# A ring of four weight and cache slots as one tile, with merged weight transfers

## The chip, the cores and the metric

The kernel runs on one core of a Trainium2 chip. The metric is the device time of one execution in microseconds; lower is better. TensorE (PE) does the matrix products, VectorE (DVE) the element-wise work, reductions and 32x32 block transposes, ScalarE (ACT) activations and copies, GpSimd (POOL) the memsets at the start, and SyncE (SP) issues almost all transfers. Sixteen DMA engines move the data from HBM to the on-chip memory.

## The reference

One decoding step for two sequences. A normalised input row feeds two branches: a windowed attention over cached keys and values (32 query heads, 8 key/value heads, a window of 4096 positions), and a small gated MLP. Their product is added to the input.

```python
xn = _layernorm(x)                                   # x: (2, 1, 512)
# attention
q = (xn @ wq).reshape(2, 1, 32, 128)                 # wq: (512, 4096)
k = k_cache[:, :, Sk - 4096:, :]                     # (2, 8, 4096, 128), each used by 4 heads
v = v_cache[:, :, Sk - 4096:, :]
p = softmax(einsum(q, k) * 128 ** -0.5)
s = einsum(p, v).reshape(2, 1, 4096) @ wo            # wo: (4096, 512)
# gated MLP
z = gelu(xn @ w_in)                                  # w_in: (512, 1792)
z1, z2 = z[..., :896], _layernorm(z[..., 896:])
g = silu((z1 * (w_sp * z2 + b_sp)) @ w_out)          # w_out: (896, 512)
return x + s * g
```

All data are float32. The keys and values in the window are 67 MB, w_q and w_o 8.4 MB each, w_in 3.7 MB and w_out 1.8 MB; each is read once.

## The kernel before

**Units.** The cache is worked in eight units (`NU`, L69): a unit is one sequence and two key/value heads, and its keys are one tile of 128 partitions by 64 positions by 128 (32 KB a partition, 4 MB), its values another. `load_unit` (L114) issues one transfer for one of them.

**The ring.** All large data go through the pool `ring` (L76), four buffers of 32 KB a partition (`SLOT`, L73). `slot` (L81) takes the next buffer in turn, and the transfer that fills it waits until every reader of the tile that was there has finished. In order of turns: w_in, w_out, the two halves of w_q, then k0, k1, v0, k2, v1, k3, v2 and so on to k7, v6, v7, and three buffers for w_o. All these transfers stand on SP, in this order; the loop at L416 issues those of the cache, the loop at L426 those of w_o.

**w_q.** Two transfers (L101 to L104), each of two of the four rows that a partition holds: 32 KB of every 64 KB. The q matmuls (L274 to L281) run over k = 0..3, eight groups of four for each k pair; those of k = 0, 1 read the first half and those of k = 2, 3 the second.

**w_o.** 32 blocks of 512 columns a partition (64 KB a partition in all). They come in pieces of 8, 8, 8, 4, 2, 1 and 1 blocks (`pieces`, L424), a transfer each; the first two pieces share one buffer, the third has one, the last four share one. After the second piece one small transfer brings `x4` (L434), which is x spread over eight partitions.

**Order of work.** Every engine runs its instructions in the order in which the program writes them (`InOrder`, L27); an instruction that waits holds up all behind it on its engine. SP holds nothing but transfers. The sequence is: layer norm and MLP branch up to `gate` (L145 to L270), the q matmuls, `qT`, `qm`, `rp` and `qbd` (L273 to L296, DVE and PE in turn), and then the loop over units (L438 to L464). In it DVE turns a unit's keys in four chunks (`turn`, tile `kt`), PE multiplies each chunk with q (`shares`, tile `sh`), ACT copies it, PE adds the shares up (`add_shares`, tile `s`); in between, for the unit before, the maximum, the exponentials (`p`), their transposes (`pT`) and the products with the values (`values`, tile `acc`) are done. So a k buffer is free after the fourth transposition of its unit, and a v buffer after the sixteen products of the next unit's turn.

**The end.** After the last unit (L465 to L477) the heads are gathered into `oT`. Then blocks 0 to 27 of w_o are multiplied into `part` (L482 to L485), ACT copies `part`, and blocks 28 to 31 go into `so` directly, with the copy added in before block 30 (L489 to L497). Two DVE operations and one store finish. In the trace an ordinary block is two matmul instructions of `part`, and one of the last four blocks is eight of `so`.

All engine calls go through one helper, so the profile gives them line 37; they are told apart by the tile that they write.

Of the kernel before, what the change touches and what calls it, by code (L numbers as in the profile page):

```python
# [9 lines left out]
F32 = mybir.dt.float32  # L10
# [4 lines left out]
P = 128  # L15
HQ, DH = 32, 128
G = 4
# [4 lines left out]
def ap(t, offset, dims):  # L22

    return bass.AP(tensor=t.tensor, offset=t.offset + offset, ap=[list(t.ap[0])] + [list(d) for d in dims])
# [18 lines left out]
def kernel(  # L43
# [14 lines left out]
    pe, dve, act, sp = (InOrder(tc, e) for e in (nc.tensor, nc.vector, nc.scalar, nc.sync))  # L58
    B, _, D = x.shape
    _, HKV, SK, _ = k_cache.shape  # L60
    W = min(4096, max(256, SK // 4))
    REP = HQ // HKV
    F = w_in.shape[1]
    FH = F // 2
    KT = D // P
    FT = FH // P
    DC = D // G
    SCALE = DH ** -0.5
    NU = B * HKV // 2  # L69
# [3 lines left out]
    SLOT = J * DH  # L73
    BANKS = {"s": 2, "sh": 2, "acc": 2, "mo": 1, "col": 1}

    ring = ctx.enter_context(tc.tile_pool(name="ring", bufs=4))  # L76
    cst = ctx.enter_context(tc.tile_pool(name="cst", bufs=1))
    sb = ctx.enter_context(tc.tile_pool(name="sb", bufs=2))
    ps = ctx.enter_context(tc.tile_pool(name="ps", bufs=1, space=bass.MemoryType.PSUM))

    def slot(name):  # L81
        return ring.tile([P, SLOT], F32, tag="slot", name=name)

    def const(name, *shape):
        return cst.tile([P, *shape], F32, tag=name, name=name)

    def bank(name, tag):
        return ps.tile([P, 512], F32, tag=tag, name=name, bufs=BANKS[tag])


    xs = cst.tile([B, D], F32, tag="xs", name="xs")
    act.dma_start(xs, x[:, 0, :])
    win = slot("win")[:, : KT * F]
    sp.dma_start(win, w_in.rearrange("(p k) f -> p (k f)", p=P))
    win = win.rearrange("p (k f) -> p k f", k=KT)
    wout = slot("wout")[:, : FT * D]
    sp.dma_start(wout, w_out.rearrange("(p j) d -> p (j d)", p=P))
    wout = wout.rearrange("p (j d) -> p j d", j=FT)
    wq_v = wq.rearrange("(p k) f -> p k f", p=P)
    wqt = []  # L100
    for a in range(2):  # L101
        t = slot(f"wq{a}")
        sp.dma_start(t, wq_v[:, 2 * a : 2 * a + 2, :].rearrange("p k f -> p (k f)"))
        wqt.append(t.rearrange("p (k f) -> p k f", k=2))  # L104

    wb1 = cst.tile([1, 2], F32, tag="wb1", name="wb1")
    act.dma_start(wb1[:, 0:1], bass.AP(tensor=w_sp.tensor, offset=w_sp.offset, ap=[[1, 1], [1, 1]]))
# [2 lines left out]
    def by_group(t):  # L110

        return bass.AP(tensor=t.tensor, offset=t.offset, ap=[[DC, G], [D, B], [1, DC]])

    def load_unit(cache, u, name):  # L114

        b, w = divmod(u, NU // B)
        t = slot(f"{name}{u}")
        first = cache[b, 2 * w, SK - W :, :]
        src = bass.AP(tensor=first.tensor, offset=first.offset, ap=[[SLOT, P // 2], [SK * DH, 2], [1, SLOT]])
        sp.dma_start(t, src)  # L120
        return t.rearrange("p (j d) -> p j d", d=DH)


    ident = const("ident", P)
# [1 line left out]
    xnT = const("xnT", KT, 32)  # L126
# [5 lines left out]
    x4 = const("x4", DC)  # L132
# [70 lines left out]
    for k in range(KT):  # L203
        for g in range(G):
            pe.matmul(
                pz[32 * g : 32 * g + 32, :], xnT[:, k, :], ap(win[:, k, :], g * FQ, [[FH, 2], [1, FQ]]),
                start=(k == 0), stop=(k == KT - 1),
            )
    wb_ps = bank("wb_ps", "mo")[:, :2]
    pe.matmul(wb_ps, ones[0:1, :], wb1, start=True, stop=True)  # L210
    wb = const("wb", 2)
# [46 lines left out]
    for j in range(FT):  # L258
        g = j % G
        pe.matmul(yp[32 * g : 32 * g + 32, :], hT[:, j, :], wout[:, j, :], start=(j < G), stop=(j >= FT - G))  # L260
    ys = sb.tile([P, D], F32, tag="shs", name="ys")
    act.activation(ys, yp, AF.Copy)
    y = bank("yq", "mo")[:, :DC]
# [9 lines left out]
    pq = [bank(f"q_ps{r}", "s") for r in range(2)]  # L273
    for k in range(KT):  # L274
        for r in range(2):
            for g in range(G):
                c = (r * G + g) * 512
                pe.matmul(
                    pq[r][32 * g : 32 * g + 32, :], xnT[:, k, :], wqt[k // 2][:, k % 2, c : c + 512],
                    start=(k == 0), stop=(k == KT - 1),  # L280
                )  # L281
    qT = sb.tile([P, 1024], F32, tag="qT", name="qT", bufs=1)
    for r in range(2):
        dve.transpose(qT[:, 512 * r : 512 * r + 512], pq[r])
# [13 lines left out]
    def q_of(u, dq):  # L298
        return ap(qbd, (u.n * 4 + dq) * 32, [[1, 32]])


    class Unit:
        pass

    def turn(u, m):

        u.kt[m] = sb.tile([P, JC, DH], F32, tag="kt", name=f"kt{u.n}_{m}", bufs=3)
        dve.transpose(
            u.kt[m].rearrange("p j d -> p (j d)"), u.k[:, JC * m : JC * m + JC, :].rearrange("p j d -> p (j d)")
        )  # L310

    def shares(u, m):

        u.sh = bank(f"sh{u.n}_{m}", "sh")
        for dq in range(4):
            pe.matmul(
                u.sh[32 * dq : 32 * dq + 32, :], q_of(u, dq), u.kt[m][:, :, 32 * dq : 32 * dq + 32],
                start=True, stop=True,
            )
        u.shs[m] = sb.tile([P, 512], F32, tag="shs", name=f"shs{u.n}_{m}")  # L320
        act.activation(u.shs[m], u.sh, AF.Copy)

    def add_shares(u, m):

        if m == 0:
            u.s = bank(f"s{u.n}", "s")
        pe.matmul(u.s, add_dq[:, NCH - 1 - m : NCH - 1 - m + P], u.shs[m], start=(m == 0), stop=(m == NCH - 1))
# [24 lines left out]
    def probs_t(u):  # L352
        u.pT = sb.tile([P, JC, 32], F32, tag="pT", name=f"pT{u.n}")
        dve.transpose(u.pT.rearrange("p j r -> p (j r)"), u.p)

    def weights(u):
        pe.matmul(u.mo[:, 32:34], same_r, u.l, start=True, stop=True)
# [8 lines left out]
    def values(u, part=0, parts=1):  # L366
        if part == 0:
            u.acc = bank(f"acc{u.n}", "acc")
        n = JC // parts
        for j in range(n * part, n * part + n):  # L370
            c = j % G
            pe.matmul(
                u.acc[32 * c : 32 * c + 32, :], u.pT[:, j, :], u.v[:, j : J : JC, :],
                start=(j < G), stop=(j >= JC - G),
            )

    def scale_out(u):
        u.o = sb.tile([P, 4, DH], F32, tag="o", name=f"o{u.n}")
        for jj in range(4):
            act.activation(  # L380
                u.o[:, jj, :], u.acc[:, jj * DH : (jj + 1) * DH], AF.Copy, scale=u.wd[:, jj : jj + 1]
            )
# [3 lines left out]
    def collect(u):  # L386

        if u.n == 0:
            col[0] = bank("col", "col")
        r = slice(32 * u.b, 32 * u.b + 32)  # L390
        pe.matmul(
            col[0][r, :], sel[:, 24 - 8 * u.w : 56 - 8 * u.w], u.o.rearrange("p j d -> p (j d)"),
            start=(u.w == 0), stop=(u.w == NU // B - 1),
        )
# [11 lines left out]
            )  # L406
        dve.tensor_copy(oT[:, :, 16 * u.b], t)

    units = []
    for n in range(NU):  # L410
        u = Unit()
        u.n, u.kt, u.shs = n, {}, {}
        u.b, u.w = divmod(n, NU // B)
        units.append(u)

    for n in range(NU + 1):  # L416
        if n < NU:
            units[n].k = load_unit(k_cache, n, "k")
        if n > 0:
            units[n - 1].v = load_unit(v_cache, n - 1, "v")  # L420

    wo_v = wo.rearrange("(p j) d -> p j d", j=32)
    blocks = []
    pieces = ((8, 8), (8,), (4, 2, 1, 1))  # L424
    j = 0
    for i, piece in enumerate(pieces):  # L426
        t = slot(f"wo{i}").rearrange("p (j d) -> p j d", d=D)
        at = 0
        for n in piece:
            sp.dma_start(t[:, at : at + n, :], wo_v[:, j : j + n, :])  # L430
            blocks += [(t, at + a) for a in range(n)]
            at, j = at + n, j + n
            if j == 16:
                sp.dma_start(x4[0:P:16, :], by_group(x))  # L434

    prev = old = None
    last = units[-1]
    for u in units:  # L438
        turn(u, 0)
        shares(u, 0)  # L440
        if old is not None:
            gather(old)
        if prev is not None:
            share_max(prev)
            probs(prev)
            weights(prev)
        turn(u, 1)
        shares(u, 1)
        add_shares(u, 0)
        if prev is not None:  # L450
            probs_t(prev)
            weigh(prev)
            if u is not last:
                values(prev)
        for m in range(2, NCH):
            turn(u, m)
            shares(u, m)
            add_shares(u, m - 1)
        if u is not last and prev is not None:
            scale_out(prev)  # L460
        add_shares(u, NCH - 1)
        if u is not last and prev is not None:
            collect(prev)
        old, prev = prev, u  # L464
    values(old, 0, 2)  # L465
    share_max(last)
    probs(last)
    values(old, 1, 2)
    weights(last)
    probs_t(last)  # L470
    weigh(last)
# [10 lines left out]
    for n in range(EARLY):  # L482
        t, a = blocks[n]
        g = n % G
# [4 lines left out]
    for n in range(EARLY, 32):  # L489
        if n == LATE:  # L490
            spread_quarters(so, parts, start=False, stop=False)
        t, a = blocks[n]
# [37 lines left out]
```

## Time and profile before

| | |
|---|---|
| time of three runs | 217.88, 218.21, 218.34 us (median 218.21) |
| the profiled execution | 217.89 us, of which the span of the trace is 216.1 us |
| mean granted clock of TensorE | 0.854 |
| read from HBM | 89.40 MB, 414 GB/s over the span |
| busy: PE, DVE, ACT | 153.6, 108.6, 44.0 us |
| SP's transfers | 3912 packets |

In the rows of the profile times are in microseconds from the start of the span, unless marked ns. `k<-in_A_k_cache_dram` is what is written and what it is read from; `x32` is a number of instructions; `128x512 f32` is partitions by elements. In the time line and the groups the brackets or the last column tell how long the engine was idle just before, and what ended that. The chain of waits is followed back from the last instruction of the span, at each step to what released it. In the page's slices a digit is the busy share in tenths, 9 for 90% or more.

### The profile page before, as it was taken

The numbers are of one execution on the slowest core, as the hardware profiler recorded it, in microseconds if no ns is written. First come the engines' busy times: TensorE is split into PE (matmuls) and PEld (weight loads), VectorE is DVE, ScalarE is ACT, GpSimd is POOL, SyncE is SP. The second block draws the span as 40 slices with busy tenths as digits, with TensorE's granted clock in tenths as the row PEclk, the third lists the DMA queues.
The fourth block names the chain that finished last, engine by engine and source line by source line (L and its number), as shares of the span: only waits on it lengthen the run. The fifth ranks groups of instructions, "written<-read, shape, count | busy, mean of one in ns | idle before, by whom it ended". The sixth has DMA issues, their size and how long they took to land.

```text
span 216.1 us, 2228 instructions
## 1 busy us (share of the span) xinstructions
PE 153.6 (71%) x866; PEld 43.1 (20%) x866; DVE 108.6 (50%) x176; ACT 44.0 (20%) x109; POOL 2.6 (1%) x14
## 2 busy tenths in 40 slices
PE   0173185518959957994995699459959967997963
PEld 0121121101212212221221222222222212231311
DVE  2505402569788079338806941685479089331001
ACT  5003310002231331043131304120331241242001
POOL 4000000000000000000000000000000000000000
PEclk9998579955997995899799589856996996999698
DMA  6999999999999999999999999999999999999990
GB/s 256 425 437 467 406 438 422 431 443 419 455 400 473 397 455 412 431 437 419 450 403 461 412 461 403 443 419 425 449 412 452 412 455 412 443 397 425 424 368 26
DMA packets 3929, 89.54 MB, mean 414 GB/s; under 512 B 446, under 2 KB 462, under 8 KB 848
## 3 DMA queue, kind: packets, MB, share of 16 engines
q1 hardware_dynamic: 3912, 89.40, 96.7%
q8 instruction: 7, 0.11, 0.2%
q10 hardware_dynamic: 8, 0.00, 0.0%
q14 instruction: 2, 0.02, 0.0%
HBM read 89.40 MB, written 0.00 MB: 414 GB/s over the span
## 4 chain that ended last, share of the span: by engine, by line
DMA 52%; PE 28%; DVE 18%; issue 1%; DVEq 0%; SPq 0%
DMA k<-in_A_k_cache_dram 38%; DVE kt L37 15%; PE sh L37 9%; PE s L37 8%; DMA wo<-in_A_wo_dram 8%; PE acc L37 6%; DMA win<-in_B_w_in_dram 5%; PE z L37 2%; PE mo L37 1%; PE so L37 1%; DVE m L37 1%; DVE pT L37 1%; PE oT L37 0%; DVE mx L37 0%; PE col L37 0%
## 5 line engine op out<-in xcount | busy, mean ns | idle before, releaser
L37 DVE STREAM_TRANSPOSE kt<-k 128x2048 f32<-128x2048 f32 x32 | 72.7, 2295 | 41.7 <-DMA k<-in_A_k_cache_dram 35.7
L37 PE MATMUL sh<-kt,qbd 128*32 128x512 f32 x256 | 41.4, 710 | 18.4 <-DVE kt L37 18.4
L37 ACT ACTIVATE shs<-sh 128x512 f32<-128x512 f32 x32 | 19.1, 597 | 119.3 <-PE sh L37 119.3
L37 PE MATMUL s<-shs,add_dq 128*128 128x512 f32 x64 | 40.0, 732 | 0.0
L37 PE MATMUL acc<-v,pT 128*32 128x512 f32 x256 | 31.9, 640 | 0.2 <-DVE pT L37 0.2
L37 PEld LDWEIGHTS s<-shs,add_dq 128*128 128x128 f32 x64 | 11.0, 215 | 30.1 <-issue 25.7
L37 PEld LDWEIGHTS sh<-kt,qbd 128*32 128x32 f32 x256 | 6.5, 115 | 38.8 <-issue 24.5
L37 PEld LDWEIGHTS acc<-v,pT 128*32 128x32 f32 x256 | 7.7, 119 | 25.5 <-issue 18.3
L37 PE MATMUL mo<-l,same_r 128*128 128x2 f32 x16 | 3.7, 299 | 10.6 <-ACT p L37 10.6
L37 ACT ACTIVATE o<-acc,wd 128x128 f32<-128x128 f32 x32 | 9.1, 372 | 3.4 <-PE acc L37 3.4
L37 PE MATMUL part<-wo,oT 128*32 128x512 f32 x56 | 8.0, 708 | 2.0 <-DMA wo<-in_A_wo_dram 1.7
L37 ACT ACTIVATE p<-s,nb 128x256 f32<-128x256 f32 x16 | 7.6, 490 | 7.2 <-DVE nb L37 6.9
L37 PE MATMUL q_ps<-wq,xnT 128*32 128x512 f32 x64 | 7.3, 594 | 2.3 <-DMA wq<-in_A_wq_dram 2.3
L37 PE MATMUL col<-o,sel 128*32 128x512 f32 x16 | 8.3, 601 | 0.4 <-ACT o L37 0.4
L37 PE MATMUL z<-win,xnT 128*32 128x448 f32 x32 | 5.3, 836 | 4.5 <-DMA win<-in_B_w_in_dram 4.5
L37 DVE TENSOR_REDUCE m<-s 128x2 f32<-128x512 f32 x8 | 5.4, 670 | 4.9 <-PE s L37 4.9
L37 DVE TENSOR_TENSOR res<-so,gate 128x128 f32<-128x128 f32 x1 | 0.3, 291 | 11.7 <-PE so L37 11.7
L37 PE MATMUL y<-wout,hT 128*32 128x512 f32 x14 | 3.3, 993 | 3.8 <-issue 3.8
L37 DVE STREAM_TRANSPOSE pT<-p 128x512 f32<-128x512 f32 x8 | 5.4, 674 | 1.2 <-ACT p L37 1.2
L37 ACT ACT_TABLE_LOAD x4 | 5.1, 1283 | 1.9 <-issue 1.9
L37 PE MATMUL xnT_ps<-ident,xn 2*128 2x2 f32 x4 | 0.6, 252 | 6.9 <-DVE xn L37 6.9
L37 PEld LDWEIGHTS mo<-l,same_r 128*128 128x128 f32 x16 | 3.0, 233 | 12.2 <-ACT p L37 12.2
(106 smaller groups left out, 63.2 us busy)
## 6 DMA issues: line engine op xcount, KB each, us to landing
k<-in_A_k_cache_dram SPq DMA_DIRECT2D x8, 4096.0 KB, 26.0
v<-in_A_v_cache_dram SPq DMA_DIRECT2D x8, 4096.0 KB, 30.6
wq<-in_A_wq_dram SPq DMA_DIRECT2D x2, 4096.0 KB, 29.7
wo<-in_A_wo_dram SPq DMA_DIRECT2D x3, 2048.0 KB
win<-in_B_w_in_dram SPq DMA_DIRECT2D x1, 3584.0 KB
wout<-in_B_w_out_dram SPq DMA_DIRECT2D x1, 1792.0 KB, 15.0
wo<-in_A_wo_dram SPq DMA_DIRECT2D x1, 1024.0 KB
wo<-in_A_wo_dram SPq DMA_DIRECT2D x1, 512.0 KB, 18.0
```

The lines of the kernel that those rows point to most:

```text
L37: return self.tc.keep_in_program_order(call(*args, **kwargs))
```

## The change

The pool `ring` is gone. One tile of 4 x 32 KB a partition, also named `ring`, takes its place, and its four parts are handed out by the program: `enqueue` appends a load with the number of parts that it needs, `advance` marks parts as free and issues loads from the head of the queue as long as their parts are free. `advance` is called behind the last reader of each part. The waits of a transfer come from the parts of the tile that earlier instructions read or wrote.

```diff
-    ring = ctx.enter_context(tc.tile_pool(name="ring", bufs=4))
...
-    def slot(name):
-        return ring.tile([P, SLOT], F32, tag="slot", name=name)
+    ring = cst.tile([P, 4 * SLOT], F32, tag="ring", name="ring")
+    free = [True] * 4
+    queue = []
+    turns = [0]
+
+    def enqueue(load, count=1):
+        at = turns[0] % 4
+        turns[0] += count
+        queue.append((load, range(at, at + count)))
+        advance()
+
+    def advance(*slots):
+        for n in slots:
+            free[n] = True
+        while queue and all(free[n] for n in queue[0][1]):
+            load, at = queue.pop(0)
+            for n in at:
+                free[n] = False
+            load(ring[:, at[0] * SLOT : (at[-1] + 1) * SLOT], at[0])
```

w_q takes two parts at once and comes in one transfer, 64 KB a partition:

```diff
-    wq_v = wq.rearrange("(p k) f -> p k f", p=P)
-    wqt = []
-    for a in range(2):
-        t = slot(f"wq{a}")
-        sp.dma_start(t, wq_v[:, 2 * a : 2 * a + 2, :].rearrange("p k f -> p (k f)"))
-        wqt.append(t.rearrange("p (k f) -> p k f", k=2))
...
+            sp.dma_start(t[:, :n], w.rearrange("(p k) f -> p (k f)", p=P))
+            weight[name] = t[:, :n].rearrange("p (k f) -> p k f", k=k)
...
+    enqueue(load_rows("in", w_in, KT))
+    enqueue(load_rows("out", w_out, FT))
+    enqueue(load_rows("q", wq, KT), 2)
```

w_o comes in pieces of 16, 8, 4, 1, 1, 1 and 1 blocks, the first of them 32 KB a partition, and `x4` in two transfers of four partitions each in place of one of eight:

```diff
-    pieces = ((8, 8), (8,), (4, 2, 1, 1))
...
-                sp.dma_start(x4[0:P:16, :], by_group(x))
...
+            if len(blocks) == 16:
+                for b in range(B):
+                    sp.dma_start(x4[16 * b : P : 32, :], x[b].rearrange("o (g c) -> (o g) c", g=G))
...
+    for piece in ((16,), (8,), (4, 1, 1, 1, 1)):
+        enqueue(load_blocks(piece))
```

The calls that hand parts back: `advance(0)` behind the matmuls of w_in, `advance(1)` behind those of w_out, `advance(2, 3)` behind the q matmuls, `advance(u.slot["k"])` ahead of a unit's last `add_shares`, `advance(prev.slot["v"])` behind it, and `advance(old.slot["v"])` at the end. The order in which loads take the parts is that of the turns before.

More of the change, by code (lines that the diff above doesn't have):

```diff
@@ L92, with load_rows, load @@
     act.dma_start(xs, x[:, 0, :])
[L93 to L98, printed above, removed]
-    wq_v = wq.rearrange("(p k) f -> p k f", p=P)
-    wqt = []
-    for a in range(2):
-        t = slot(f"wq{a}")
-        sp.dma_start(t, wq_v[:, 2 * a : 2 * a + 2, :].rearrange("p k f -> p (k f)"))
-        wqt.append(t.rearrange("p (k f) -> p k f", k=2))
+    weight = {}
+    def load_rows(name, w, k):
+        def load(t, at):
+            n = k * w.shape[1]
+            sp.dma_start(t[:, :n], w.rearrange("(p k) f -> p (k f)", p=P))
+            weight[name] = t[:, :n].rearrange("p (k f) -> p k f", k=k)
+        return load
+    enqueue(load_rows("in", w_in, KT))
+    enqueue(load_rows("out", w_out, FT))
+    enqueue(load_rows("q", wq, KT), 2)
+    win, wout, wqt = (weight[n] for n in ("in", "out", "q"))
     wb1 = cst.tile([1, 2], F32, tag="wb1", name="wb1")
@@ L114, in load_unit, with load, load_blocks @@
     def load_unit(cache, u, name):
-        b, w = divmod(u, NU // B)
-        t = slot(f"{name}{u}")
-        first = cache[b, 2 * w, SK - W :, :]
+        first = cache[u.b, 2 * u.w, SK - W :, :]
         src = bass.AP(tensor=first.tensor, offset=first.offset, ap=[[SLOT, P // 2], [SK * DH, 2], [1, SLOT]])
-        sp.dma_start(t, src)
-        return t.rearrange("p (j d) -> p j d", d=DH)
+        def load(t, at):
+            sp.dma_start(t, src)
+            setattr(u, name, t.rearrange("p (j d) -> p j d", d=DH))
+            u.slot[name] = at
+        return load
+    class Unit:
+        pass
+    units = []
+    for n in range(NU):
+        u = Unit()
+        u.n, u.kt, u.shs, u.slot = n, {}, {}, {}
+        u.b, u.w = divmod(n, NU // B)
+        units.append(u)
+    for n in range(NU + 1):
+        if n < NU:
+            enqueue(load_unit(k_cache, units[n], "k"))
+        if n > 0:
+            enqueue(load_unit(v_cache, units[n - 1], "v"))
+    wo_v = wo.rearrange("(p j) d -> p j d", j=32)
+    blocks = []
+    def load_blocks(piece):
+        def load(t, at):
+            t = t.rearrange("p (j d) -> p j d", d=D)
+            a = 0
+            for n in piece:
+                j = len(blocks)
+                sp.dma_start(t[:, a : a + n, :], wo_v[:, j : j + n, :])
+                blocks.extend((t, a + i) for i in range(n))
+                a += n
+            if len(blocks) == 16:
+                for b in range(B):
+                    sp.dma_start(x4[16 * b : P : 32, :], x[b].rearrange("o (g c) -> (o g) c", g=G))
+        return load
+    for piece in ((16,), (8,), (4, 1, 1, 1, 1)):
+        enqueue(load_blocks(piece))
     ident = const("ident", P)
@@ L208 @@
             )
+    advance(0)
     wb_ps = bank("wb_ps", "mo")[:, :2]
@@ L260 @@
         pe.matmul(yp[32 * g : 32 * g + 32, :], hT[:, j, :], wout[:, j, :], start=(j < G), stop=(j >= FT - G))
+    advance(1)
     ys = sb.tile([P, D], F32, tag="shs", name="ys")
@@ L278 @@
                 pe.matmul(
-                    pq[r][32 * g : 32 * g + 32, :], xnT[:, k, :], wqt[k // 2][:, k % 2, c : c + 512],
+                    pq[r][32 * g : 32 * g + 32, :], xnT[:, k, :], wqt[:, k, c : c + 512],
                     start=(k == 0), stop=(k == KT - 1),
                 )
+    advance(2, 3)
     qT = sb.tile([P, 1024], F32, tag="qT", name="qT", bufs=1)
@@ L299, in q_of @@
         return ap(qbd, (u.n * 4 + dq) * 32, [[1, 32]])
-    class Unit:
-        pass
     def turn(u, m):
@@ L407, in gather @@
         dve.tensor_copy(oT[:, :, 16 * u.b], t)
[L409 to L423, printed above, removed]
-    pieces = ((8, 8), (8,), (4, 2, 1, 1))
[L425 to L433, printed above, removed]
-                sp.dma_start(x4[0:P:16, :], by_group(x))
     prev = old = None
@@ L460 @@
             scale_out(prev)
+        advance(u.slot["k"])
         add_shares(u, NCH - 1)
         if u is not last and prev is not None:
+            advance(prev.slot["v"])
             collect(prev)
@@ L468 @@
     values(old, 1, 2)
+    advance(old.slot["v"])
     weights(last)
```

## The prediction

> **What bounds the kernel now.** I read the page first (busy shares, slices, queues, chain), then the transfers by stage, then the chain in order of time and the time line around the edited places.
>
> ```profile
> span 216.1 us, 2228 instructions
> PE 153.6 (71%) x866; PEld 43.1 (20%) x866; DVE 108.6 (50%) x176; ACT 44.0 (20%) x109; POOL 2.6 (1%) x14
> DMA  6999999999999999999999999999999999999990
> q1 hardware_dynamic: 3912, 89.40, 96.7%
> q8 instruction: 7, 0.11, 0.2%
> DMA 52%; PE 28%; DVE 18%; issue 1%; DVEq 0%; SPq 0%
> ```
>
> No compute engine is above 71%; the 16 DMA engines are in the top tenth in every slice but the first and the last, and SP's queue (q1) alone fills 96.7% of them. The next rows are stretches of the span; the last column is GB/s, the one before it the DMA share.
>
> ```profile
> 1.80:37.40 35.60, 14.66 (x100) 5.22 (x102) 11.07 (x51) 7.62 (x12) 1.38 (x5) 0.86 1.01 431
> 37.40:76.00 38.60, 28.32 (x150) 7.03 (x150) 24.70 (x31) 6.75 (x16) 0.00 (x0) 0.82 0.99 427
> 114.50:153.00 38.50, 28.46 (x151) 8.36 (x149) 23.27 (x28) 6.67 (x18) 0.00 (x0) 0.78 1.01 434
> 192.60:202.40 9.80, 8.07 (x54) 2.90 (x58) 1.76 (x6) 2.28 (x8) 0.00 (x0) 0.91 1.00 425
> 202.40:207.40 5.00, 3.94 (x32) 0.91 (x28) 0.00 (x0) 0.00 (x0) 0.00 (x0) 0.83 0.98 412
> ```
>
> Weights, caches and w_o all move at 412 to 434 GB/s, at a share of 0.98 to 1.01. The kernel is one continuous stream of 89.40 MB, and an edit pays only if it changes the bytes, the rate or the ends, or lets the stream run dry. The chain tells how far it is from that:
>
> ```profile
> 69.46 25.97 DMA k<-in_A_k_cache_dram
> 107.54 26.75 DMA k<-in_A_k_cache_dram
> 193.00 18.05 DMA wo<-in_A_wo_dram
> ```
>
> The load of k3 lands at 69.46 + 25.97 = 95.43 and that of k5 at 107.54 + 26.75 = 134.29. From one to the other are four transfers of 4 MB, so one takes 38.86 / 4 = 9.72 us. A load handed over at 69.46 that lands 25.97 later stood behind 25.97 - 9.72 = 16.2 us of queued work: that much delay in handing out a slot is free there. At 193.00, where the short w_o pieces are handed over, the last piece that the chain follows lands 18.05 later, and these pieces themselves take only some 4 us.
>
> **The change, part by part.**
>
> *The ring as one tile.* In the changed kernel's instruction order PE, DVE, ACT and POOL run the same operations in the same sequence, and SP fills the same slots in the same order: win 0, wout 1, w_q 2 and 3, k0 0, k1 1, v0 2, k2 3, v1 0, and so on. A cache load still waits for the last reader of its own slot, transposes for a k, matmuls into acc for a v; some transposes name an older load beside their own, long landed. Cost: 0.
>
> *w_q as one transfer.* No q matmul starts before all 8 MB are there. Rows of the time line (start, duration, operation, idle time before it), and at the end one of the waits (in total, times, longest):
>
> ```profile
> 31.43 3.62 PE L37 MATMUL q_ps<-wq,xnT 128*32 128x512 f32 x32
> 35.10 0.54 SPq L37 DMA_DIRECT2D v<-in_A_v_cache_dram  x1
> 37.36 3.64 PE L37 MATMUL q_ps<-wq,xnT 128*32 128x512 f32 x32 [2.32 <-DMA wq<-in_A_wq_dram]
> 41.06 0.54 SPq L37 DMA_DIRECT2D k<-in_A_k_cache_dram  x1
> 44.21 1.66 DVE L37 TENSOR_SCALAR qbd<-rp,grpm 128x256 f32<-128x256 f32 x4 [1.03 <-PE rp L37]
> 46.89 8.89 DVE L37 STREAM_TRANSPOSE kt<-k 128x2048 f32<-128x2048 f32 x4 [1.02 <-DMA k<-in_A_k_cache_dram]
> 56.70 2.31 DVE L37 STREAM_TRANSPOSE kt<-k 128x2048 f32<-128x2048 f32 x1 [0.92 <-DMA k<-in_A_k_cache_dram]
> DVE kt L37 <- DMA k<-in_A_k_cache_dram: 35.7, 7, 7.5
> ```
>
> The q matmuls end at 37.36 + 3.62 + 3.64 = 44.6 instead of 41.0, 3.6 late; PE is now idle ahead of them, and if they begin with a stretch of 3.4 us at half clock (such stretches stand under rival A), 1.7 more. Behind them stand the load of v0 (35.10 becomes 41 to 43), that of k2 (41.06 becomes 45 to 46) and, on DVE, which runs in order, qT, qm, qbd and the first transposes. qbd ended at 45.87 and will end at 49.5 to 51.2; the transposes of k0, landed by 46.89, start 2.6 to 4.3 late. It is covered: k0 and k1 keep the queue busy until about 56.7, so v0 and k2 have some 11 us to spare; DVE waits 35.7 us for k in 7 waits, 5.1 each, and swallows 4.3 within two units; the loads behind are handed over at most 4.3 later, out of 16. On the path: 0. Without the cover it would be 2.6 to 4.3.
>
> *Longer rows.* In the tail each matmul group starts on a landing, which gives the price by row length:
>
> ```profile
> 201.23 5.04 PE L37 MATMUL part<-wo,oT 128*32 128x512 f32 x32 [0.35 <-issue]
> 207.34 1.92 PE L37 MATMUL part<-wo,oT 128*32 128x512 f32 x16 [1.06 <-DMA wo<-in_A_wo_dram]
> 209.85 1.07 PE L37 MATMUL part<-wo,oT 128*32 128x512 f32 x8 [0.59 <-DMA wo<-in_A_wo_dram]
> 211.05 0.60 ACT L37 ACTIVATE parts<-part 128x512 f32<-128x512 f32 x1 [13.14 <-PE part L37]
> 211.09 0.65 PE L37 MATMUL so<-wo,oT 128*32 128x128 f32 x16 [0.17 <-DMA wo<-in_A_wo_dram]
> ```
>
> The piece of four blocks (1 MB, 8 KB a partition) took 209.85 - 207.34 = 2.51, that of two (0.5 MB, 4 KB) 211.09 - 209.85 = 1.24. A fixed price of a queued transfer would be 2 x 1.24 - 2.51 = -0.03: none. Per 4 MB that is 10.04 us in rows of 8 KB, 9.92 in rows of 4 KB, and 9.72 (above) in rows of 32 KB. So two doublings, 8 KB to 32 KB, gain up to 0.32 per 4 MB. Rows of 64 KB do not occur. For w_q I bound the doubling by the whole 0.32 per 4 MB, so -0.64, and on the other side by its rows being cut up and going like those of 8 KB, +0.64; for w_o's first sixteen blocks (16 KB to 32 KB) by -0.32 and 0. I take -0.1 for w_q and -0.1 for w_o: a price per row halves with each doubling, so little is left beyond 32 KB.
>
> *The last pieces* (8, 8, 8, 4, 2, 1, 1 become 16, 8, 4, 1, 1, 1, 1). The two-block piece becomes two of 2 KB rows: 0 to +0.1, taken as +0.04 (0.32 x 0.5 MB / 4 MB). One more issue on SP, some 0.5 us, early. The last piece now waits on SP for the landing of the sixteen blocks, where it waited for v7's; behind it on SP is only the store of the result. The sixteen land at 207.34 - 2 x 2.51 = 202.3, and the queue then still holds fifteen blocks, over 8 us: hidden; uncovered, an issue of 0.5 and a start of about as much.
>
> *x in two transfers.* 4 KB of 89.40 MB, and one short issue more on SP with over 10 us of queue behind it: taken as +0.03.
>
> The sum is -0.1 - 0.1 + 0.04 + 0.03 = -0.13 on the profiled execution's 217.89 us (span 216.1), so 217.76. That execution lies 0.32 under the median of the three runs, 218.21; against that median the sum gives 218.1.
>
> **The rivals.**
>
> *A, slower: the end of PE's work takes over.* The sixteen-block transfer lands as a whole. Before, the first eight blocks were there and PE began at 201.23; now it begins at 202.2, on the far side of a gap. The rows below are stretches of 3.41 us: start and end, length, PE busy, granted clock, DMA share, GB/s; the last two are of the time line.
>
> ```profile
> 81.28:84.69 3.41, 2.53 (x11) 0.50 1.01 432
> 84.69:88.10 3.41, 3.41 (x10) 0.51 0.89 384
> 142.71:146.13 3.41, 2.74 (x11) 0.50 1.00 432
> 146.13:149.54 3.41, 3.41 (x14) 0.51 1.03 442
> 101.75:105.17 3.41, 3.02 (x10) 0.51 0.89 384
> 105.17:108.58 3.41, 3.41 (x30) 1.00 0.95 406
> 200.74:204.15 3.41, 3.06 (x18) 0.51 1.01 427
> 204.15:207.57 3.41, 2.35 (x24) 1.00 0.95 398
> 211.70 0.43 PE L37 MATMUL so<-parts,rowm 128*32 128x128 f32 x8
> 211.94 0.84 PE L37 MATMUL so<-wo,oT 128*32 128x128 f32 x16
> ```
>
> After 2.53 and 2.74 busy at half clock the next stretch stays at half, after 3.02 and 3.06 it is full. Starting at 202.2, PE would be busy about 2.0 of the stretch that ends at 204.15, so the next would stay at half until 207.57. A matmul of this group takes 1.92 / 16 = 0.12 at full clock, 0.24 at half: 22 are done by 207.57, 10 more by 208.8, the next 16 by 210.7, 8 by 211.7 (210.9 before), the copy by 212.4, and the last matmuls, 0.43 + 0.84 after it, by 213.7 instead of 211.94 + 0.84 = 212.8: +0.9, so with a little of the sum's gain left 219.0. It decides once the 48 matmuls end after 209.85; if the clock comes back at 204.15 they are done with 32 by 207.0, ahead of the next landing, and nothing is lost. Against it: where the stretches fall need not be the same in each execution; by stepping their border through 3.41 us about a third of the positions are bad.
>
> [...]
>
> *B, faster: long rows are worth the whole bound.* -0.64 - 0.32 + 0.07 = -0.9, so 217.3. Against it: the best stage of the trace moves 434 GB/s; the weights' stage, at 431, would gain only 35.6 x 3 / 434 = 0.25 by reaching it.
>
> *C, either way: which DMA engine is last.* The instruction fetches take 0.2% of 16 engines' span, 6.9 us in 7 packets, 1.0 each, and each holds up one engine while 15 go on. A transfer lands with its slowest engine. With the early PE work moved, the first fetch can fall on another engine: 1.0 sooner or later at most, more likely half: 217.6 or 218.6.
>
> *D, not what it says:* the 64 KB rows are cut into rows of 32 KB. Then w_q gains nothing and 218.2 is left; it goes with the forecast.
>
> **How the numbers follow.** A measurement of this kernel tells about 0.2% (0.44 us) from no change. Forecast (with D) 0.60, A 0.18, B 0.09, C 0.13 in equal halves. The forecast's own range is 217.6 to 218.6, from the runs' spread of 0.46 and the two row bounds; it reaches past the 0.2% with 0.07 below and 0.04 above. Faster: 0.07 + 0.09 + 0.06 = 0.22. Slower: 0.04 + 0.18 + 0.06 = 0.28. Same: the remaining 0.50. The range takes in B's and A's times: 217.3 to 219.0.
>
> **What would show it.** The q matmuls start once, as 64, after 35, and the first transposes of k0 at 49 to 51; from the third k on DVE waits for the landing again and the loads land 9.7 apart. The DMA share stays at 0.97 or more to 202. The part matmuls start on a w_o landing near 202.2 and the last so matmuls still start on a landing (forecast) or right behind the copy of the parts (A). I would be wrong if a slice in the middle fell below 9, if w_q landed more than 0.6 earlier or later for the same bytes, or if the tail behind the last landing grew.

## The result, and the profile after

| | before | changed |
|---|---|---|
| median of 11 runs each, us | 218.02 (217.59 to 218.66) | 218.85 (218.50 to 219.06) |
| ratio of the times | | 1.0034, 95% interval 1.0021 to 1.0046 |
| span of the profiled execution, us | 216.1 | 216.9 |

The changed kernel is slower by 0.34%, some 0.8 us, where no change was forecast. First the page of the changed kernel, its busy slices, queues and chain:

```profile
span 216.9 us, 2230 instructions
...
DMA  7998897999999999999999999999999999999980
...
q1 hardware_dynamic: 3772, 89.40, 96.3%
q8 instruction: 7, 0.11, 0.2%
q14 instruction: 3, 0.02, 0.0%
...
DMA 70%; PE 17%; DVE 10%; issue 1%; SPq 0%; DVEq 0%
```

The stream looks as before: the same bytes in 140 packets fewer. Some slices stand lower: the 4th and 5th and the last but one at 8, the 7th at 7. The early ones come from the way of counting. A slice is given the whole of every packet that starts in it, and w_q's packets of 64 KB took 2.4 us each; the 3rd and the 6th slice, just ahead, show 532 and 545 GB/s, and when each packet is spread over its own time all of these slices stand at 1.00. The last but one reaches further past the end of the stream, since the span is longer. There are two instructions more in the span, 2230 for 2228. The stages, in stretches of the span (the last two columns are DMA share and GB/s), and then the chain of waits:

```profile
1.80:37.40 35.60, 12.12 (x72) 4.55 (x76) 11.07 (x51) 7.62 (x12) 1.38 (x5) 0.80 1.00 427
114.50:153.00 38.50, 29.47 (x154) 8.58 (x154) 23.27 (x28) 7.59 (x23) 0.00 (x0) 0.82 1.01 434
202.40:207.40 5.00, 3.81 (x36) 1.27 (x40) 0.00 (x0) 0.00 (x0) 0.00 (x0) 1.00 0.96 405
```

```profile
1.62 34.48 DMA ring<-in_A_wq_dram
...
72.39 23.05 DMA ring<-in_A_k_cache_dram
...
107.55 26.75 DMA ring<-in_A_k_cache_dram
...
212.30 0.47 PE so L37 x8
212.80 0.30 DVE res L37
213.12 0.29 DVE res L37
```

The load that ends at 72.39 + 23.05 = 95.44 is k3's, and 107.55 + 26.75 = 134.30 is k5's; before they landed at 95.43 and 134.29. At the end of the stream the changed kernel is even 0.05 ahead: its last `so` matmuls start at 212.30 and its last DVE operation at 213.12. Before, the chain said:

```profile
212.35 0.47 PE so L37 x8
212.84 0.30 DVE res L37
213.17 0.29 DVE res L37
```

So everything up to 213.4 is as fast as before, and the span is 0.8 longer. All of the loss lies behind the last operation, in the store of the result. The queue of SP, as issued (time line) and waited for at the end (waits), before and after:

```profile
213.49 0.61 SPq L37 DMA_DIRECT2D out_dram<-res  x1
...
SPq L525 <- DMA out_dram<-res: 0.7, 1, 0.7
```

```profile
213.44 0.59 SPq L37 DMA_DIRECT2D out_dram<-res  x1
...
SPq L560 <- DMA out_dram<-res: 1.7, 1, 1.7
```

The 4 KB of the result are issued 0.05 earlier, and SP waits 1.0 longer for them. In the trace the store lands 1.69 us after its issue before (213.49 to 215.18) and 2.65 after (213.44 to 216.09). What else moves at that time is seen in three stretches at the end, before and then changed (DMA share and GB/s last; a packet is counted where it starts):

```profile
213.50:214.60 1.10, 0.00 (x0) 0.00 (x0) 0.00 (x0) 0.00 (x0) 0.00 (x0) 0.89 0.00 0
214.60:215.30 0.70, 0.00 (x0) 0.00 (x0) 0.00 (x0) 0.00 (x0) 0.00 (x0) 0.50 0.02 6
215.30:216.90 1.60, 0.00 (x0) 0.00 (x0) 0.00 (x0) 0.00 (x0) 0.00 (x0) 0.50 0.02 5
```

```profile
213.50:214.60 1.10, 0.00 (x0) 0.00 (x0) 0.00 (x0) 0.00 (x0) 0.00 (x0) 0.73 0.03 7
214.60:215.30 0.70, 0.00 (x0) 0.00 (x0) 0.00 (x0) 0.00 (x0) 0.00 (x0) 0.50 0.02 6
215.30:216.90 1.60, 0.00 (x0) 0.00 (x0) 0.00 (x0) 0.00 (x0) 0.00 (x0) 0.50 0.00 0
```

The middle stretch holds the store, 6 GB/s x 0.7 us = 4 KB, in both. Besides it some 8 KB move (5 x 1.6 = 8 KB, 7 x 1.1 = 7.7 KB): before behind the store (in the trace at 216.76, behind the end of the span), after just ahead of it. That is a packet of queue q14, an instruction fetch: three of them are 0.02 MB, 8 KB each. In the trace of the changed kernel it starts at 214.58 and takes 569 ns on one DMA engine. Six of the store's eight packets of 512 bytes start from 214.68 to 214.73, and the other two at 215.15 and 215.17, right when the fetch is over; three of the store's four landing events come at 215.10 and 215.11, the fourth at 216.09. That late start makes some 0.4 of the 0.96. The rest comes behind it: the last small packet of the store, 4 bytes, starts at 214.84 before and at 215.20 after, and the landing follows 0.34 later before and 0.90 later after. What holds it back there no run shows.

Which instruction calls for the fetch? The order of DVE's instructions, with their numbers, tells what the change did to it. The first transposition of k0 and of k1, before on the left and after on the right (the numbers count DVE's operations alone; DMAHW and a number is the semaphore of a transfer):

```
58 kt_0<-k     [waits DMAHW7]                    58 kt_0<-ring  [waits DMAHW6, DMAHW1]
62 kt_0<-k     [waits DMAHW0, DVE, PE]           62 kt_0<-ring  [waits DMAHW4, DMAHW7, DVE, PE]
```

k0 lies in the part where w_in was, k1 in the part where w_out was, and each first reader now also waits for that older load. The added wait stands in an instruction of its own, so DVE's recorded instructions (operations, waits, drains) go from 192 to 194. PE has one more and SP one fewer, ACT and POOL as many as before; together that makes the two more of the page.

That gives theory F, for fetch: DVE fetches 8 KB when it gets to its 191st recorded instruction, and some 1.1 to 1.5 us later the packet runs. Before, the 191st stands at the closing barrier, behind the store. With two more instructions the 191st is the drain right behind the last operation, and its fetch meets the store. The rivals in the expectations put the loss into the transfers, the waits of the ring themselves or the clock at the end.

### The profile page after: what moved, and what is told of

The parts are those of the page before. It is cut to its first block, busy times and chain, and to the rows that moved or that the text cites. A ratio compares the mean times of both kernels' runs of the same rounds, so it can differ in the third digit from the quotient of the medians.

```text
span 216.9 us, 2230 instructions
## 1 busy us (share of the span) xinstructions
PE 153.2 (71%) x866; PEld 42.9 (20%) x866; DVE 108.5 (50%) x176; ACT 44.0 (20%) x109; POOL 2.6 (1%) x14
## 4 chain that ended last, share of the span: by engine, by line
DMA 70%; PE 17%; DVE 10%; issue 1%; SPq 0%; DVEq 0%
DMA ring<-in_A_k_cache_dram 34%; DMA ring<-in_A_wo_dram 20%; DMA ring<-in_A_wq_dram 16%; DVE kt L37 8%; PE q_ps L37 4%; PE acc L37 4%; PE sh L37 4%; PE s L37 3%; PE mo L37 1%; PE oT L37 0%; PE col L37 0%; SPq L37 0%; DVE res L37 0%; DVE pT L37 0%; DVE m L37 0%
## 5 line engine op out<-in xcount | busy, mean ns | idle before, releaser
L37 DVE STREAM_TRANSPOSE kt<-ring 128x2048 f32<-128x2048 f32 x32 | 72.5, 2294 | 35.6 <-DMA ring<-in_A_k_cache_dram 25.8
L37 PE MATMUL s<-shs,add_dq 128*128 128x512 f32 x64 | 40.7, 742 | 0.0
L37 PE MATMUL acc<-ring,pT 128*32 128x512 f32 x256 | 31.9, 639 | 0.2 <-DVE pT L37 0.2
L37 PEld LDWEIGHTS acc<-ring,pT 128*32 128x32 f32 x256 | 7.7, 117 | 26.1 <-issue 18.3
L37 PE MATMUL q_ps<-ring,xnT 128*32 128x512 f32 x64 | 8.9, 721 | 4.8 <-DMA ring<-in_A_wq_dram 4.8
L37 PE MATMUL part<-ring,oT 128*32 128x512 f32 x56 | 6.6, 597 | 3.3 <-DMA ring<-in_A_wo_dram 3.3
L37 PE MATMUL z<-ring,xnT 128*32 128x448 f32 x32 | 5.1, 810 | 4.2 <-DMA ring<-in_B_w_in_dram 4.2
L37 DVE STREAM_TRANSPOSE qT<-q_ps 128x512 f32<-128x512 f32 x2 | 1.4, 717 | 10.8 <-PE q_ps L37 10.7
L37 PE MATMUL y<-ring,hT 128*32 128x512 f32 x14 | 3.2, 969 | 3.8 <-issue 3.8
```

What stands on the lines that cost most here:

```text
L37: return self.tc.keep_in_program_order(call(*args, **kwargs))
```

## The experiments

All were timed in five rounds against the kernel before on the same chip; the three groups share their runs of it (medians 217.95, 218.13 and 217.93). The table has what the traces show; the fetch is the last on q14.

| kernel | DVE instructions | the 191st starts | fetch starts | store, issue to landing | time, us | ratio (95%) |
|---|---|---|---|---|---|---|
| before | 192 | 215.60 | 216.76 | 1.69 | 218.02 | |
| changed | 194 | 213.14 | 214.58 | 2.65 | 218.85 | 1.0034 (1.0021 to 1.0046) |
| b_plus2 | 194 | 213.41 | 214.88 | 2.72 | 219.04 | 1.0049 (1.0031 to 1.0067) |
| b_plus1 | 193 | 215.68 | 217.06 | 1.69 | 218.32 | 1.0016 (1.0005 to 1.0028) |
| a_minus2 | 192 | 215.30 | 216.44 | 1.69 | 217.91 | 0.9995 (0.9984 to 1.0006) |
| a_plus2 | 196 | 212.49 | 213.91 | 1.98 | 218.17 | 1.0005 (0.9994 to 1.0017) |
| ring_only | 194 | 213.41 | 214.84 | 2.49 | 218.95 | 1.0037 (1.0021 to 1.0054) |
| tail_only | 192 | 215.76 | 216.91 | 1.69 | 217.98 | 0.9994 (0.9984 to 1.0004) |
| a_minus4 | 190 | none | 217.15 | 1.69 | 217.79 | 0.9987 (0.9977 to 0.9996) |
| b_minus4 | 188 | none | 218.62 | 1.72 | 218.40 | 1.0013 (1.0000 to 1.0026) |
| ring_minus4 | 190 | none | 217.29 | 1.70 | 217.88 | 1.0002 (0.9990 to 1.0013) |
| b_minus2 | 190 | none | 217.23 | 1.71 | 217.93 | 0.9998 (0.9985 to 1.0010) |

### Two instructions more on the kernel before (b_plus2), and one (b_plus1)

Two copies of 128 x 4 numbers that nobody reads, at the start of the kernel, where DVE waits for w_in in any case. Nothing of the ring or of the transfers is changed.

```diff
+    for i in range(2):
+        dve.tensor_copy(const(f"spare{i}", G), grpm)
```

> The kernel before with two small copies more on DVE (128x4, into tiles that nobody reads) among the set-up work at 9 us, where DVE then idles until 17.7 us. Theory F (fetch): the change put two waiting instructions more on DVE, and with them DVE's last instruction fetch of 8 KB falls on the store of the result; so this kernel, with none of the transfers changed, gets slower by about 0.8 us like the change (ratio near 1.0035), and its trace has an 8 KB fetch about 1 us behind the last DVE operation, with the store landing 2.6 us after its issue instead of 1.7. Theory T (transfers): the loss comes from the merged or split transfers; so this kernel stays within 0.2 us of before, its store as before.

The time was 219.04, 1.1 over the kernel before, where 0.8 was expected; the interval of its ratio overlaps with that of the changed kernel. Stretches at the end of it, and SP's wait for the store:

```profile
213.70:214.85 1.15, 0.00 (x0) 0.00 (x0) 0.00 (x0) 0.00 (x0) 0.00 (x0) 1.00 0.00 0
214.85:215.50 0.65, 0.00 (x0) 0.00 (x0) 0.00 (x0) 0.00 (x0) 0.00 (x0) 0.68 0.08 19
...
SPq L527 <- DMA out_dram<-res: 1.8, 1, 1.8
```

19 GB/s x 0.65 us = 12 KB: fetch and store in one stretch. The loss of the changed kernel is there without any part of the change.

> The kernel before with one small copy more on DVE at the same place. Theory F: the fetch is set off by one fixed instruction of DVE's stream; one more instruction makes this the wait at the end barrier, still behind the store, so no change (within 0.2 us). Theory T: no change either. A theory that each instruction more costs time by itself expects half of the loss of two.

With one copy the 191st instruction is still at the barrier, the fetch stays behind the store, and SP's wait is the old one:

```profile
SPq L527 <- DMA out_dram<-res: 0.7, 1, 0.7
```

The time, 218.32, is 0.37 over the kernel before, a small miss of F. In its trace DVE spends 0.48 us from the 191st instruction to the 192nd, both of the barrier; the same two take 0.11 before. That may be the 0.37, but it is one trace. By its time alone this run doesn't exclude a price for each instruction added, half of b_plus2's loss for one; the store, at its old 1.69, and the next two kernels speak against it.

### Two fewer on the changed kernel (a_minus2), and two more (a_plus2)

In a_minus2 the constants are built with two instructions fewer, with the same values:

```diff
-    for a in range(2):
-        dve.tensor_copy(
-            ap(add_dq, NCH - 1 + 16 * a, [[32, G], [4, REP]]),
-            rowm[:, 16 * a : 16 * a + 16].rearrange("p (g h) -> p g h", g=G),
-        )
+    dve.tensor_copy(
+        ap(add_dq, NCH - 1, [[16, 2], [32, G], [4, REP]]),
+        rowm.rearrange("p (a g h) -> p a g h", a=2, g=G),
+    )
...
-    for a in range(2):
-        dve.tensor_mul(spot[:, a], ap(grpm, 0, [[1, G], [0, NCH]]), ap(diag, 0, [[0, G], [1, NCH]]))
-        dve.tensor_scalar_mul(spot[:, a], spot[:, a], am[:, a : a + 1])
+    dve.tensor_mul(spot[:, 0], ap(grpm, 0, [[1, G], [0, NCH]]), ap(diag, 0, [[0, G], [1, NCH]]))
+    for a in (1, 0):
+        dve.tensor_scalar_mul(spot[:, a], spot[:, 0], am[:, a : a + 1])
```

> The changed kernel with two DVE instructions fewer in the set-up: the two copies into add_dq are one, and spot is made with one product less; the same values. Theory F: DVE's stream has the length of before again, the fetch falls behind the end, and the time is that of before or 0.1 less (217.9 to 218.1). Theory T: it stays at 218.85, since these instructions lie where DVE idles.

The loss is gone: 217.91, a ratio of 0.9995 where the changed kernel has 1.0034. The ring, its waits and all transfers are those of the change.

a_plus2 is the changed kernel with the two idle copies of b_plus2 added.

> The changed kernel with two small DVE copies more in the set-up. Theory F: the fetch is set off two instructions earlier, ahead of the last operation, so it is over (or nearly so) when the store's packets run: faster than the change, 218.0 to 218.4, though it has more work. Theory T: 218.85 or more.

More work than in the changed kernel, and yet 1.0005. Its last stretches and the wait for the store:

```profile
213.60:214.30 0.70, 0.00 (x0) 0.00 (x0) 0.00 (x0) 0.00 (x0) 0.00 (x0) 1.00 0.03 12
214.30:215.30 1.00, 0.00 (x0) 0.00 (x0) 0.00 (x0) 0.00 (x0) 0.00 (x0) 1.00 0.02 4
...
SPq L562 <- DMA out_dram<-res: 1.1, 1, 1.1
```

Some 8 KB (12 x 0.7) are now through by 214.3 and the store's 4 KB follow. The 191st instruction is the wait ahead of the last operation, so the fetch has moved in front. No rival that puts the cost into transfers or ring waits makes a kernel faster by added work; F does.

### The parts of the change alone (ring_only, tail_only)

ring_only is the one tile with its parts, but with w_q in two halves, w_o in the old pieces and `x4` in one transfer. tail_only is the kernel before with the new pieces and `x4` in two:

```diff
-    pieces = ((8, 8), (8,), (4, 2, 1, 1))
+    pieces = ((16,), (8,), (4, 1, 1, 1, 1))
...
-                sp.dma_start(x4[0:P:16, :], by_group(x))
+                for b in range(B):
+                    sp.dma_start(x4[16 * b : P : 32, :], x[b].rearrange("o (g c) -> (o g) c", g=G))
```

ring_only, against the changed kernel:

```diff
-    enqueue(load_rows("q", wq, KT), 2)
+    enqueue(load_half(0))
+    enqueue(load_half(1))
...
-    for piece in ((16,), (8,), (4, 1, 1, 1, 1)):
+    for piece in ((8, 8), (8,), (4, 2, 1, 1)):
```

> The changed kernel with all its transfers undone (w_q in two halves, w_o in pieces of 8, 8, 8, 4, 2, 1, 1, x in one): only the ring as one tile is left, and with it the two waiting instructions more on DVE. Theory F (fetch on the store): slower than before by the whole loss, 218.6 to 219.0, with the fetch of 8 KB at 1.4 us behind the start of DVE's last instruction. Theory T (transfers): 218.0, like before.

> The kernel before with the tail's transfers of the change (w_o in pieces of 16, 8, 4, 1, 1, 1, 1, x in two), the ring pool and w_q as before; DVE's stream is as long as before. Theory F: 217.8 to 218.1, no difference from before. Theory T, or the prediction's rival A (PE's end takes over because the first eight blocks of w_o come later): 218.4 to 219.

ring_only has the whole loss, 218.95 against 218.13, and tail_only none, 217.98. Stretch and wait at the end of ring_only:

```profile
214.60:215.30 0.70, 0.00 (x0) 0.00 (x0) 0.00 (x0) 0.00 (x0) 0.00 (x0) 1.00 0.06 18
...
SPq L570 <- DMA out_dram<-res: 1.5, 1, 1.5
```

Again fetch and store together, 18 x 0.7 = 12.6 KB. tail_only is also a look at rival A of the prediction. A stretch of it, and rows of its time line:

```profile
204.00:206.00 2.00, 2.00 (x16) 0.71 (x12) 0.00 (x0) 0.00 (x0) 0.00 (x0) 0.50 0.92 389
...
202.46 7.05 PE L37 MATMUL part<-wo,oT 128*32 128x512 f32 x48 [1.76 <-DMA wo<-in_A_wo_dram]
...
209.81 1.07 PE L37 MATMUL part<-wo,oT 128*32 128x512 f32 x8 [0.29 <-DMA wo<-in_A_wo_dram]
```

At full clock 48 matmuls take 5.8 (1.92 for 16); here they took 7.05, with the clock at 0.50 from 204 to 206, and were done at 209.5, just before the next landing. So the half clock did come, and cost nothing in this execution.

### Four fewer (a_minus4, b_minus4), and which of it is the count (ring_minus4, b_minus2)

If fewer instructions put the fetch off, four fewer should keep it clear of the store by a margin. Two more copies are moved to GpSimd:

```diff
-    dve.tensor_copy(sel[:, 24:32], rowr)
-    dve.tensor_copy(place[:, 3 : 3 + P : 4], rowm)
+    nc.gpsimd.tensor_copy(sel[:, 24:32], rowr)
+    nc.gpsimd.tensor_copy(place[:, 3 : 3 + P : 4], rowm)
```

together with the edit of a_minus2; a_minus4 has it on the changed kernel, b_minus4 on the kernel before.

> The changed kernel with four DVE instructions fewer: the two merged ones, and the copies into sel and place on POOL, which is idle. DVE's stream then has 190 traced instructions and never comes to the 191st, at which the fetch was set off. Theory F: no third fetch of 8 KB at all, and neither the store nor the end barrier waits for one: 217.7 to 217.9, the same as with two fewer or 0.1 to 0.2 less. Theory T: 218.85.

> The kernel before with the same four DVE instructions fewer (188 traced). Theory F: the fetch that stood behind the store is gone too; before lost at most 0.1 us to it at the end barrier, so 217.8 to 218.0, no difference that can be measured. If DVE's set-up copies were on the path, it would be faster by their time, 0.6 us.

a_minus4 took 217.79, against 218.13 of the kernel before. It is the only version that is faster than the kernel before by an interval that leaves out 1, and only just: the ratio is 0.9987, and 0.13% is less than the 0.2% taken for the resolution. The 8 KB still come, at 217.15, behind the end of the span; that no third fetch would come was not exact.

b_minus4 was expected below 218.13 and took 218.40. Its profile is not about the fetch, which is far behind the store. Stretches around 208, and two rows of the time line:

```profile
206.00:208.00 2.00, 0.49 (x4) 0.20 (x8) 0.00 (x0) 0.00 (x0) 0.00 (x0) 0.87 0.96 397
208.00:210.00 2.00, 2.00 (x12) 0.39 (x8) 0.00 (x0) 0.00 (x0) 0.00 (x0) 0.50 0.96 376
210.00:212.00 2.00, 2.00 (x26) 0.66 (x22) 0.00 (x0) 0.00 (x0) 0.00 (x0) 0.77 0.38 144
...
207.50 4.44 PE L37 MATMUL part<-wo,oT 128*32 128x512 f32 x24 [2.47 <-DMA wo<-in_A_wo_dram]
...
213.66 0.29 DVE L37 TENSOR_TENSOR res<-so,gate 128x128 f32<-128x128 f32 x1 [12.33 <-PE so L37]
```

The granted clock is at half from 208 to 210, 24 `part` matmuls take 4.44 us instead of 2.99 (1.92 + 1.07), and the first `res` operation comes at 213.66 instead of 212.84. That is the mechanism of rival A, +0.8 at the end, in a kernel with the old pieces. The trace is of the second slowest of twelve executions (218.83); that this makes the median's 0.27 over the kernel before is not shown.

Two runs ask whether the lower count by itself does harm or good: ring_only with the edit of a_minus4, and the kernel before with that of a_minus2.

> The ring as one tile alone, with every transfer as before, and four DVE instructions fewer (the two merged ones, and the copies into sel and place on POOL), so that DVE's fetch falls behind the end. Theory F: the ring by itself costs nothing, 217.9 to 218.3, against 218.95 for the same kernel with these four instructions. A theory that the ring's extra waits delay the transposes by themselves expects it to stay above 218.6. Theory C (clock at the end): w_o comes here in pieces of 8, 8, so PE ends its first sixteen blocks 2 us ahead of the next landing; in some executions the clock is halved there and the tail is 0.8 us longer, so single times spread over about 1 us, where the kernels with sixteen blocks in one piece spread over 0.5.

> The kernel before with the two merged set-up instructions of DVE (190 traced, two fewer). Theory F: nothing to gain, since the fetch is already behind the store: 217.8 to 218.3. If fewer DVE instructions cost time by themselves (four fewer gave 218.40), it lies at 218.2 to 218.4. Theory C: a wide spread of single times, about 1 us, as in the kernel before.

217.88 and 217.93 against 217.93: neither. ring_minus4 has the ring as one tile, with its two added waits, and takes the time of the kernel before. So the waits cost nothing; where they put the fetch costs 0.8.

## Why the prediction was wrong, and where it held

**What failed.** The step is "*The ring as one tile*": "some transposes name an older load beside their own, long landed. Cost: 0." The waits are over when they are met, and that part is right (ring_minus4: 1.0002). But two of them came as instructions of their own on DVE. The step counted operations and left out that an added wait can lengthen DVE's program (192 recorded instructions became 194), and that an instruction fetch can hold up data, as here the store: two of its packets start at 215.15 and 215.17, when the fetch from 214.58 is over after 0.57. Measured, the term is +0.8 (ring_only against its kernel before: 218.95 - 218.13), not 0. By the two profiles: the store takes 0.96 longer, starts 0.05 earlier, and the span grows by 0.8.

**Rival C** named instruction fetches, but the wrong ones: those of q8, in the stream, for which it priced a DMA engine that is last. The fetch that decided is of q14, behind the stream. Its price of 1.0 for a fetch was near, but it looked for it on the landing of a load and not on that of the store. In the stream a fetch did move a landing, and the time did not follow: before, the first one of q8 runs from 35.17 to 36.23, and of the sixteen landing events of w_q's second half fifteen come by 35.87 and the last at 37.32. In the five kernels whose first 16 KB of q8 start at 34.0 to 35.5, w_q lands at 36.9 to 37.6 (before: 35.17 and 37.32); in the other seven they start at 36.5 or later, and it lands at 35.7 to 36.1 (changed: 40.06 and 36.11). Yet k0 lands at 46.87 before and at 46.88 in the changed kernel.

**The stream**, as forecast, was not touched. The landings of k3 and k5 (95.44, 134.30) and the last `so` group (212.30, 0.05 earlier; forecast 0.13) are above. The chance that long rows are worth much (B) is out: w_q's stage moved 427 GB/s where it was 431, the middle 434 in both. Its landing 1.2 earlier is not the long rows' work: three of the seven kernels under C that land as early have w_q in two halves. That the 64 KB rows are cut up (D) is out too: the trace has 128 packets of 64 KB, one for each row. What these transfers are worth by themselves stays within the resolution: tail_only 0.9994, a_minus2 0.9995, a_minus4 0.9987.

**w_q as one transfer** went by the steps of the sum. Rows of the changed kernel's time line:

```profile
36.15 8.92 PE L37 MATMUL q_ps<-ring,xnT 128*32 128x512 f32 x64 [4.78 <-DMA ring<-in_A_wq_dram]
...
41.71 0.54 SPq L37 DMA_DIRECT2D ring<-in_A_v_cache_dram  x1
...
45.14 0.54 SPq L37 DMA_DIRECT2D ring<-in_A_k_cache_dram  x1
...
48.12 1.66 DVE L37 TENSOR_SCALAR qbd<-rp,grpm 128x256 f32<-128x256 f32 x4 [0.86 <-PE rp L37]
...
49.69 11.07 DVE L37 STREAM_TRANSPOSE kt<-ring 128x2048 f32<-128x2048 f32 x5
```

64 matmuls, started 1.2 earlier than the sum had them (36.15 for 37.36), in 8.92 instead of 2 x 3.63: the stretch at half clock came (granted 0.50 from 36.15 to 39.90), 1.7 as said. v0 is issued at 41.71 and k2 at 45.14 (forecast 41 to 43 and 45 to 46), `qbd` ends at 49.8 (49.5 to 51.2), the transposes start at 49.69. By 95 nothing is left of it.

**Rival A** did not decide here: the sixteen blocks' matmuls started at 202.42 (forecast 202.2) and ran at full clock (granted 1.00 from 200.74 to 207.57), as the rows show, so that the next piece was waited for.

```profile
202.42 3.64 PE L37 MATMUL part<-ring,oT 128*32 128x512 f32 x32 [1.53 <-DMA ring<-in_A_wo_dram]
...
207.23 1.92 PE L37 MATMUL part<-ring,oT 128*32 128x512 f32 x16 [1.17 <-DMA ring<-in_A_wo_dram]
...
209.72 1.06 PE L37 MATMUL part<-ring,oT 128*32 128x512 f32 x8 [0.56 <-DMA ring<-in_A_wo_dram]
```

Its threshold, the 48 matmuls done by 209.85, agrees with tail_only (done at 209.5, no loss), which tries one side of it. Its price was met where nobody looked for it, in b_minus4. Whether the new pieces make it rarer is open: single times spread with a standard deviation of 0.28 to 0.36 us in five kernels with pieces of 8 and 8 (b_plus2, with eight runs, 0.46; ring_only, with seven, 0.19), and of 0.13 to 0.21 in four with sixteen in one (a_plus2: 0.31). It was not tried with the clock alone.

**Of the signs of being wrong** that were named, two more showed beside the decisive one: w_q landed 1.2 earlier, and slices ahead of the middle fell below 9. Both are explained above, by the fetch of q8 (twelve traces side by side, no run with that alone changed) and by the counting of packets, and neither reached the end. The decisive one is "if the tail behind the last landing grew". From the start of the last `so` group to the end of the span it was 216.1 - 212.35 = 3.75 and is 216.9 - 212.30 = 4.6.

## What to carry to other kernels

When an edit should cost nothing and costs a little, look behind the last operation first: compare issue and landing of the last store, and what the instruction queues move in that microsecond. Here two added waits became two instructions (192 to 194), and a count that was off by two put a fetch onto the store (2.65 us from issue to landing for 1.69, and 2.72 in b_plus2). Add or remove two idle instructions at the start to tell such an accident from a real cost, before the edit is judged (b_plus2 1.0049, a_plus2 1.0005). And in the one tile whose parts are handed out, the new reader of a part waited for its old load as well (DVE's operations 58 and 62), here as an instruction of its own.

## What the runs showed of the hardware

- DVE's fetch of 8 KB started 1.1 to 1.5 us after its 191st recorded instruction in all eight kernels that have a 191st, whether that was a drain or a wait of the barrier, the drain behind the last operation or a wait ahead of it. It took 0.31 to 0.57 us in those of them whose fetch ran ahead of or with the store. When it met the store, the store took 0.8 to 1.0 longer; when it ran just ahead (a_plus2), 0.3. The rule is read from the end of the kernel alone: for the two fetches of q14 in the stream (at 30 to 37 and at 107 to 109) no number of an instruction gives a distance that is the same within 2 us.
- q8 and q14 carry instructions alone (in the changed kernel 7 packets, 0.11 MB, and 3 packets, 0.02 MB). q8's first fetch started at 35.17 before and at 40.06 after, and w_q landed at 37.32 and 36.11; k0 landed at 46.87 and 46.88. With a fetch on the last store the runs were some 0.8 us of 218 longer (ring_only 218.95 for 218.13).
- Two packets out of eight were enough: in the changed kernel the last ones started 0.42 us behind the others (215.15 against 214.73), and the landing came 0.96 later. The other half of that stands between the last packet and the landing, and its cause is open. In a_plus2, where the fetch was over before the store's packets started, this part alone grew, from 0.34 to 0.63.
